# Attention with beacon tokens and a two-layer MLP on one core: products that nobody reads from the first microsecond, v loads that cast, x of one batch transposed by pairs

## The chip, the cores and the metric

The kernel runs on 1 core of one Trainium2 chip. The metric is the device time of one execution in microseconds (us), here from the first to the last thing that the core does for the program. Lower is better. TensorE (PE in the profile, PEld for its weight loads) multiplies, ScalarE (ACT) makes exponentials and copies, VectorE (DVE) and GpSimd (POOL) work elementwise, and DMA transfers are issued from the queues of SyncE (SP), ACT and POOL.

## What is computed

Inputs are float32. Attention runs over 8 batches (B) and 8 heads (H) with 576 queries (S) of width 64 (D). 16 beacon keys and values (Nb), which every query sees, stand ahead of the 576 causal ones. Its output goes through an MLP with a squared ReLU, 512 to 2048 to 512.

```python
k_all = np.concatenate([beacon_k, k], axis=2)
v_all = np.concatenate([beacon_v, v], axis=2)
scores = np.matmul(q, k_all.transpose(0, 1, 3, 2)) / np.sqrt(D)
scores = np.where(causal, -1000000000.0, scores)      # beacons are never masked
a = np.exp(scores - scores.max(-1, keepdims=True))
a /= a.sum(-1, keepdims=True) + 1e-09
x = np.matmul(a, v_all).transpose(0, 2, 1, 3).reshape(B * S, H * D)   # 4608 x 512
h = np.maximum(x @ w_in, 0.0)
out = (h * h) @ w_out
```

## The kernel before

**Tiling.** Heads go in pairs (`HP` = 4 pairs a batch, 32 in all), since two heads of 64 fill the 128 partitions of `qT` and `kT`. The 592 keys of a batch are five tiles (`NT`) of 128, the last of 80. For a pair, scores are made transposed (keys on the partitions) by L764 into PSUM, exponentials go by ACT into `pt` (L781), the diagonal is masked on DVE (L799, L803), and L819 multiplies with `vb`, which has a column of ones beside each head's v, so that the sum of a row comes with the product. DVE divides by it (`norm`, L834 and L835) into `xn`, tokens on the partitions. `xn` is transposed into `xT`, a ring of four batches with the 512 features on the partitions: batch 0 on TensorE with a copy behind (`add_xt_pe`, L883), all others by DMA transposes on SP (`add_xt`, L866), five a batch, each over one tile of tokens and all four pairs, after the norms of all four pairs.

**MLP.** Nine chunks of 512 tokens. First layer L947 (`s1`: 16 blocks of 128 hidden units, four products each), ReLU on ACT or DVE (L964, L966), square on DVE (L973); second layer L987 (`s2`, 16 products for each of four blocks of tokens), copy to `osb` by ACT, store on SP. Chunk 0 needs batch 0 alone, and its first layer is cut at token 240, so that the first two tiles of batch 0 can start it. Chunk 1 needs batch 1 as well.

**Loads.** k and q of batches 0 to 2 (`add_strided`) come by DMAs on POOL's queue that also cast to bf16 (L599), but for pair 0 of batch 0, which comes in float32 into space of `g` (L592). Each partition gets six neighbouring rows, so the data have to be turned: for batch 1, batch 2 and that first pair a copy (`spin`, on DVE; for the first pair on DVE or ACT) reorders a pair's k or q into `spare` or `qk_area`, then TensorE transposes (L635, L638) and DVE and ACT copy into `kT` and `qT` (`ek`, `eq`). Later batches use plain loads on SP, a cast on POOL and DMA transposes. v goes in float32 into one of eight staging tiles `stg` and is cast into `vb` (L439, on POOL but for two that may go to DVE); most of these loads go by SP, those in `SOFT_V` (batch 0's tiles 3 and 4, all five of batch 1) by POOL's queue (L483, L484). `w_in` (L908) and `w_out` (L917) come in four quarters each on POOL's queue, with a cast.

**The order.** The whole program is written out by a planner (`Order.run`, L155). Every piece of work is an `Op` with an engine or a choice of engines, a duration (by hand, in us), a priority, and what it needs. The planner walks through modelled time: an engine that is free takes the ready op of the least priority value for which PSUM banks (pool `ps`, eight) and other slots are free; DMA queues are modelled by packets (`Rings`). What it decides is each engine's instruction order and which engine takes an op with a choice; on the chip semaphores keep the needs, and each engine runs its list in order. `TURNS` (L306) fixes the order of POOL's loads. `gate` holds attention pairs of batch 1 and later back by the MLP's progress.

**Filler.** Where the planner finds nothing for PE between 10 and 22 us of its own time (`FILL`) and a bank is free, it adds two products of the identity `ident` into that bank, which nobody reads (`filler`, L526; in the trace L533 and L537). Their shape follows the mode of the op before: `rows` (64 rows, as the scores), `columns`, or full.

Of the kernel before, what the change touches and what calls it, by code (L numbers as in the profile page):

```python
# [129 lines left out]
class Order:  # L130
# [5 lines left out]
    FILL = (10.0, 22.0)  # L136
# [18 lines left out]
    def run(self):  # L155
# [27 lines left out]
        while events:  # L183
# [27 lines left out]
            while again:  # L211
                again = False
                for e in engines:
# [33 lines left out]
                    if best is None and e == "PE" and self.filler is not None and self.FILL[0] <= now < self.FILL[1]:  # L247
                        spot = self.pools["ps"].oldest()
                        if spot is not None:
                            best = self.filler(spot, mode or "full")  # L250
                            self.ops.append(best)
                            avail[e].append(best)
# [58 lines left out]
def kernel(  # L311
# [29 lines left out]
    def sb(name, shape, dt):  # L341
        return pool.tile(shape, dt, name=name)
# [21 lines left out]
    vb = [sb(f"vb{i}", [128, NT, H, D + 1], BF16) for i in range(2)]  # L364
# [19 lines left out]
    def act(n):  # L384
        return 0.066 + n / 1200.0
# [18 lines left out]

    nc.vector.memset(warm, 0.0)
# [46 lines left out]
    def t_start(t):  # L452
        return max(0, 128 * t - Nb)

    NPE = 3
    NXPE = 1
    SOFT_V = [(0, 3), (0, 4)] + [(1, c) for c in range(NT)]
# [10 lines left out]
    def add_load(b, x, c, prio, behind=[], sync=[]):  # L468
# [8 lines left out]
        queue = nc.gpsimd if soft else nc.sync  # L477

# [47 lines left out]
    def filler(spot, mode):  # L526


        def emit(e):
            for i in range(2):  # L530
                half = slice(64 * i, 64 * i + 64)
                if mode == "rows":
                    nc.tensor.matmul(ps[:, spot, 0:128], ident[0:64, :], ident[0:64, :], start=True, stop=True)  # L533
                elif mode == "columns":
                    nc.tensor.matmul(ps[half, spot, 0:128], ident[:, half], ident, start=True, stop=True)
                else:
                    nc.tensor.matmul(ps[:, spot, 0:128], ident, ident, start=True, stop=True)  # L537

        op = Op("fill", "PE", 0.11, emit, mode=mode)
        op.left, op.held = 0, None  # L540
        return op
# [38 lines left out]
    def add_strided(b, prio):  # L580
# [26 lines left out]
        for pr in range(HP):  # L607
# [34 lines left out]
            tp = add(f"tp{b}.{pr}", "PE", 0.55 if turned else 1.0, emit_tp, prio=100.0 * (HP * b + pr) - 190,  # L642
# [16 lines left out]
            eq = add(f"eq{b}.{pr}", ("DVE", "ACT"), {"DVE": 0.68, "ACT": 0.55}, emit_q, prio=-199.0, deps=[tp])  # L659
# [133 lines left out]
    def add_phase(b, pr, p, n, ph, take_pt, exps):  # L793
# [16 lines left out]
        def emit_av(e):  # L810
            P = pt[take_pt.held[0]]
            a = pair(av)
            for hj in range(2):
                h = 2 * pr + hj
                for t in tl:
                    for c in range(t + 1):
# [5 lines left out]
                            vb[b % 2][0:rr, c, h, :],  # L822
# [8 lines left out]
        def emit_norm(e):  # L831
# [4 lines left out]
                out=xn[b % 2].rearrange("p t (h d) -> p h t d", d=D)[:, 2 * pr:2 * pr + 2, tl[0]:tl[0] + nt],  # L836
# [8 lines left out]
        norm_ops[p, n] = add(f"norm{p}.{n}", "DVE", 0.21 + 0.137 * nt, emit_norm, prio=base - 150, deps=deps, give=av)  # L845
# [26 lines left out]

    def add_xt_pe(b):
        for k, ph in enumerate(phases(b)):
            for pr in range(HP):
# [14 lines left out]
                def emit_ev(e, pr=pr, box=box, lo=lo, hi=hi):  # L890
# [5 lines left out]
                        {"ACT": act(hi - lo), "DVE": 0.06 + (hi - lo) / 1600.0}, emit_ev, prio=-110.0,  # L896
# [164 lines left out]
    for b in range(B):  # L1061
# [32 lines left out]
        if b < NXPE:  # L1094
            add_xt_pe(b)
        else:
            add_xt(b)
# [12 lines left out]
    named["ld1v0"].behind.append(named["cast0v4"])  # L1110
# [32 lines left out]
```

## Time and profile before

| | |
|---|---|
| time, median of 3 runs | 338.75 us (338.75 to 340.36) |
| profiled execution | 338.65 us; span from first to last instruction 336.9 us |
| first matmul | 5.80 us after the span's start |
| first product of the MLP (L947) | 19.59 us |
| packets moved | 138211 DMA packets, 50.38 MB, mean 150 GB/s |
| q1 (SP's transfers) and q0 (POOL's) | 57.7% and 16.3% of 16 DMA engines' span |

The page gives for each engine its busy time; a busy PE is not PE at its peak, since matmuls overlap and their ends are modelled. A matmul's own length is therefore longer than the step from one to the next; how fast PE runs is read from the length of a run of equal matmuls. Times of rows count from the start of the span.

### The profile page before, as it was taken

Reading aid. Unit: us, or ns where it says so; the run is one execution under the profiler, and the core shown is the slowest. Engines: PE = TensorE matmul, PEld = TensorE weight load, DVE = VectorE, ACT = ScalarE, POOL = GpSimd, SP = SyncE. Lnnn points to the kernel's source line nnn. Section 1 sums busy time; section 2 is a strip of 40 time slices with the busy share of each in tenths; the row PEclk is TensorE's granted clock in tenths of the full one; section 3 lists DMA queues with packets and bytes.
Section 4 is the critical chain, followed back from the end, with each engine's and each line's share of the span. In section 5 each row is a group of like instructions: output and inputs, shape, how many; then the busy total and the mean of one; then the engine's idle time right before and its main releaser. Section 6 shows DMA issues by size and latency. Waiting matters only on the chain.

```text
span 336.9 us, 7692 instructions
## 1 busy us (share of the span) xinstructions
PE 327.1 (97%) x3172; PEld 184.2 (55%) x3172; DVE 160.5 (48%) x323; ACT 193.6 (57%) x300; POOL 86.8 (26%) x135
## 2 busy tenths in 40 slices
PE   3999999999999999999999999999999999999995
PEld 2778766545545555554468845545554544444444
DVE  6669977267604761475245632673246503301400
ACT  3887974597457647465656745755656226515611
POOL 7765911425122605140512351220000000000000
PEclk9999999999999999999999999999999999999999
DMA  9999999699959999799989996991310041011003
GB/s 167 196 207 210 206 203 207 147 247 179 221 104 223 241 199 176 185 208 228 206 121 257 242 210 138 209 196 32 104 62 2 14 120 63 0 62 64 0 17 110
DMA packets 138211, 50.38 MB, mean 150 GB/s; under 512 B 124176, under 2 KB 133264, under 8 KB 138176
## 3 DMA queue, kind: packets, MB, share of 16 engines
q1 hardware_dynamic: 128304, 40.42, 57.7%
q0 software_dynamic: 9520, 9.11, 16.3%
q8 instruction: 25, 0.41, 0.6%
q10 hardware_dynamic: 352, 0.36, 0.4%
q14 instruction: 10, 0.08, 0.1%
HBM read 37.22 MB, written 9.44 MB: 138 GB/s over the span
## 4 chain that ended last, share of the span: by engine, by line
PE 93%; DMA 2%; POOL 1%; DVE 1%; issue 1%; ACT 0%; POOLq 0%
PE ps L947 37%; PE ps L987 36%; PE ps L819 9%; PE ps L764 8%; DMA qk_area<-in_q_dram 2%; PE ps L635 1%; PE ps L1030 1%; POOL qk_area L599 1%; PE ps L883 1%; DVE g L966 0%; PE ps L537 0%; POOL vb L439 0%; PE ps L533 0%; POOL w_in L908 0%; DVE g L973 0%
## 5 line engine op out<-in xcount | busy, mean ns | idle before, releaser
L947 PE MATMUL ps<-xT,w_in 128*128 128x512 bf16 (+3 forms) x704 | 133.7, 340 | 0.2
L987 PE MATMUL ps<-w_out,g 128*128 128x512 bf16 x560 | 128.4, 379 | 0.0
L781 ACT ACTIVATE pt<-ps 128x1024 bf16<-128x1024 f32 (+3 forms) x128 | 102.9, 874 | 18.3 <-PE ps L764 18.1
L947 PEld LDWEIGHTS <-w_in 128*128 128x128 bf16 x704 | 65.9, 98 | 55.2 <-issue 3.9
L964 ACT ACTIVATE g<-ps 128x512 bf16<-128x512 f32 (+2 forms) x116 | 65.5, 568 | 39.1 <-PE ps L947 38.6
L987 PEld LDWEIGHTS <-g 128*128 128x128 bf16 x560 | 52.1, 98 | 61.1 <-issue 3.6
L973 DVE TENSOR_TENSOR g<-g 128x1024 bf16<-128x1024 bf16 (+2 forms) x80 | 52.1, 654 | 69.6 <-ACT g L964 69.4
L437 ACT COPY osb<-ps 128x512 f32<-128x512 f32 (+2 forms) x37 | 21.3, 576 | 68.8 <-PE ps L987 54.6
L439 POOL CAST qk_area<-stg 128x512 bf16<-128x512 f32 (+2 forms) x50 | 34.2, 688 | 67.5 <-DMA stg<-in_q_dram 41.0
L439 POOL CAST vb<-stg 128x512 bf16<-128x512 f32 (+1 forms) x39 | 26.1, 675 | 63.3 <-DMA stg<-in_v_dram 63.2
L799 DVE TENSOR_TENSOR pt<-pt,tri 128x1024 bf16<-128x1024 bf16 (+1 forms) x36 | 23.5, 654 | 34.2 <-ACT pt L781 34.2
L819 PEld LDWEIGHTS <-pt 128*128 128x128 bf16 (+1 forms) x960 | 34.2, 98 | 6.3 <-ACT pt L781 0.4
L966 DVE TENSOR_SCALAR g<-ps 128x512 bf16<-128x512 f32 (+2 forms) x44 | 26.8, 611 | 19.7 <-PE ps L947 19.4
L819 PE MATMUL ps<-vb,pt 128*128 128x65 bf16 (+1 forms) x960 | 35.6, 195 | 0.4 <-POOL vb L439 0.3
L764 PE MATMUL ps<-qT,kT 64*128 64x80 bf16 (+6 forms) x680 | 32.9, 235 | 0.0
L764 PEld LDWEIGHTS <-kT 64*128 64x128 bf16 x680 | 19.0, 96 | 16.8 <-issue 13.8
L835 DVE TENSOR_TENSOR xn<-ps,rcp 128x640 bf16<-128x640 f32 (+2 forms) x36 | 27.0, 750 | 1.8 <-DVE rcp L834 0.5
L834 DVE RECIPROCAL rcp<-ps 128x10 f32<-128x10 f32 (+2 forms) x36 | 7.5, 209 | 28.9 <-PE ps L819 28.9
L437 ACT COPY qT<-ps 128x576 bf16<-128x576 bf16 x12 | 7.6, 644 | 8.4 <-PE ps L635 7.4
L803 DVE TENSOR_TENSOR pt<-pt,tri 80x160 bf16<-80x160 bf16 x32 | 11.1, 347 | 0.0
L439 DVE COPY kT<-ps 128x576 bf16<-128x576 bf16 x12 | 8.9, 751 | 1.8 <-PE ps L638 1.2
L635 PE MATMUL ps<-ident,sparek 96*128 96x96 bf16 x18 | 1.5, 229 | 5.8 <-DVE sparek L439 5.8
(52 smaller groups left out, 80.4 us busy)
## 6 DMA issues: line engine op xcount, KB each, us to landing
out_dram<-osb SPq DMA_DIRECT2D x17, 512.0 KB, 3.6
stg<-in_v_dram SPq DMA_DIRECT2D x20, 256.0 KB, 5.1
stg<-in_q_dram SPq DMA_DIRECT2D x20, 256.0 KB, 5.5
stg<-in_k_dram SPq DMA_DIRECT2D x15, 256.0 KB, 4.3
w_in<-in_moe_w_in_dram POOLq DMA_DIRECT2D x4, 512.0 KB, 8.8
w_out<-in_moe_w_out_dram POOLq DMA_DIRECT2D x4, 512.0 KB, 11.6
stg<-in_v_dram SPq DMA_DIRECT2D x7, 224.0 KB, 4.5
qk_area<-in_k_dram POOLq DMA_DIRECT2D x4, 288.0 KB, 11.5
```

What stands on the lines that cost most here:

```text
L437: nc.scalar.copy(dst, src)
L439: eng[e].tensor_copy(dst, src)
L764: nc.tensor.matmul(st[:, hj, lo + col:lo + col + t1 - t0], kT[x.b % 2][hp, x.pr, 128 * c:128 * c + 128], qT[x.b % 2][hp, x.pr, t0:t1], sta ...
L781: nc.scalar.activation(pt[x.take_pt.held[0]][:, :, off:off + width], pair(box["qk"], k)[:, :, lo:lo + width], AF.Exp, bias=0.0, scale=scale)
L799: nc.vector.tensor_tensor(out=d, in0=d, in1=tri[:, m0:m0 + m, :][:, None].to_broadcast([128, 2, m, 128]), op=ALU.min)
L819: nc.tensor.matmul(a[:, hj, (t - tl[0]) * (D + 1):(t - tl[0] + 1) * (D + 1)], P[0:rr, hj, o:o + 128], vb[b % 2][0:rr, c, h, :], start=(c = ...
L835: nc.vector.tensor_tensor(out=xn[b % 2].rearrange("p t (h d) -> p h t d", d=D)[:, 2 * pr:2 * pr + 2, tl[0]:tl[0] + nt], in0=a[:, :, :, 0:D ...
L947: nc.tensor.matmul(h[:, lo - spans[0][0]:hi - spans[0][0]], w_in_sb[:, mc, ft * 128:(ft + 1) * 128], xT[:, mc, lo % RING:lo % RING + hi - lo],
L964: nc.scalar.activation(dst, h, AF.Relu, bias=0.0, scale=1.0)
L966: nc.vector.tensor_scalar(out=dst, in0=h, scalar1=0.0, scalar2=None, op0=ALU.max)
L973: nc.vector.tensor_tensor(out=d, in0=d, in1=d, op=ALU.mult)
L987: nc.tensor.matmul(o, G[:, fc, ts * 128:(ts + 1) * 128], w_out_sb[:, fc, :], start=(fc == 0), stop=(fc == NFT - 1))
```

## The change

1. `FILL` begins at 0.6 us of the planner's time. Before 2.6 us the filler is one product of 512 columns on `hot`, a part of `xT` set to zero by a memset that goes ahead of all others on DVE; it writes bank 7. After that it is the two products on `ident`, planned at 0.22 us before 6.0 us and at 0.11 us later. The form on 64 rows is gone: behind scores, it takes the full one.
2. Durations of the planner: ACT's copies and exponentials 0.105 + n / 1190 instead of 0.066 + n / 1200, the transposes of batch 0's pairs 0.55 instead of 1.0, `norm`, `eq` and `xte` by a few hundredths.
3. The loads in `SOFT_V` write bf16 straight into `vb`: no staging tile, no cast behind. A head's v and ones take 66 columns in `vb` instead of 65, of which L819 still reads 65. The rule that ties load 1v0 behind the cast of 0v4 goes with that cast.
4. Batch 1 (`XPAIR`): `xn` is laid out by pairs, and each pair's x is transposed after its own norm by three DMA transposes (tile 0, tiles 1 to 3, tile 4), twelve in all instead of five.
5. Batch 2's turning copies go to POOL instead of DVE, planned at 0.85 us instead of 0.45.

```diff
-    FILL = (10.0, 22.0)
+    FILL = (0.6, 22.0)
...
-    vb = [sb(f"vb{i}", [128, NT, H, D + 1], BF16) for i in range(2)]
+    vb = [sb(f"vb{i}", [128, NT, H, D + 2], BF16) for i in range(2)]
...
-        return 0.066 + n / 1200.0
+        return 0.105 + n / 1190.0
...
+    hot = xT[:, 0, 0:512]
+    nc.vector.memset(hot, 0.0)
     nc.vector.memset(warm, 0.0)
...
+        if soft:
+            def emit_soft(e):
+                to = vb[b % 2][:, c, :, 0:D]
+                insts = []
+                if lo:
+                    insts.append(queue.dma_start(out=to[0:Nb], in_=beacon[b].transpose([1, 0, 2])))
+                insts.append(queue.dma_start(out=to[lo:rows], in_=t[b, :, t0:t0 + rows - lo, :].transpose([1, 0, 2])))
+                return insts
+            ld = add(f"ld{b}{x}{c}", "POOL", 1.3 if lo else 0.65, emit_soft, prio=prio, dma=1.25 * rows / 128, packet=0.29,
+                     behind=load_chain[-1:] + behind, sync=sync)
+            load_chain.append(ld)
+            cast[b, x, c] = ld
+            return
...
-    def filler(spot, mode):
+    def filler(spot, mode, now):
+        mode = "columns" if mode == "columns" else "full"
+        if now < 2.6:
+            def emit(e):
+                nc.tensor.matmul(ps[:, 7, :], hot[:, 0:128], hot, start=True, stop=True)
+            op = Op("fill", "PE", 0.43, emit)
+            op.left, op.held = 0, None
+            return op
...
-                if mode == "rows":
-                    nc.tensor.matmul(ps[:, spot, 0:128], ident[0:64, :], ident[0:64, :], start=True, stop=True)
-                elif mode == "columns":
+                if mode == "columns":
...
-        op = Op("fill", "PE", 0.11, emit, mode=mode)
+        op = Op("fill", "PE", 0.22 if now < 6.0 else 0.11, emit, mode=mode)
...
-                    spin[x].append(add(f"spin{b}{x}{pr}", "DVE" if b else ("DVE", "ACT"), 0.45 if b else 0.85, emit_spin,
+                    spin[x].append(add(f"spin{b}{x}{pr}", ("POOL" if b == 2 else "DVE") if b else ("DVE", "ACT"), {"POOL": 0.85, "DVE": 0.45} if b else 0.85, emit_spin,
...
-            tp = add(f"tp{b}.{pr}", "PE", 0.55 if turned else 1.0, emit_tp, prio=100.0 * (HP * b + pr) - 190,
+            tp = add(f"tp{b}.{pr}", "PE", 0.55, emit_tp, prio=100.0 * (HP * b + pr) - 190,
...
-                out=xn[b % 2].rearrange("p t (h d) -> p h t d", d=D)[:, 2 * pr:2 * pr + 2, tl[0]:tl[0] + nt],
+                out=xn_of(b)[:, tl[0]:tl[0] + nt, pr, :].rearrange("p t (h d) -> p h t d", d=D),
...
+    def xn_of(b):
+        if b == XPAIR:
+            return xn[b % 2].rearrange("p t w -> p (t w)").rearrange("p (g t d) -> p t g d", g=HP, t=NT)
+        return xn[b % 2].rearrange("p t (g d) -> p t g d", g=HP)
+
+    def add_xt_pairs(b):
+        at = (b * S) % RING
+        for pr in range(HP):
+            for n, (lo, hi) in enumerate(((0, 1), (1, 4), (4, 5))):
+                t0, rows = t_start(lo), t_rows(lo)
+                cols = t_start(hi - 1) + t_rows(hi - 1) - t0
+                def emit(e, pr=pr, lo=lo, hi=hi, t0=t0, rows=rows, cols=cols):
+                    area = xn[b % 2].rearrange("p t w -> p (t w)")
+                    dst = xT[:, pr, at + t0:at + t0 + cols]
+                    if hi - lo > 1:
+                        dst = dst.rearrange("p (t r) -> p t r", r=rows)
+                    nc.sync.dma_start(out=dst, in_=area[0:rows, 128 * (NT * pr + lo):128 * (NT * pr + hi)], transpose=True)
+                o = add(f"xt{b}.{pr}.{n}", "SP", 0.55 + 0.19 * (hi - lo), emit, prio=-50.0 + b,
+                        deps=[norm_ops[HP * b + pr, 0]] + ring_deps(b * S + t0, b * S + t0 + cols), dma=0.16 * cols / 128,
+                        margin=1.0)
...
-            add_xt(b)
+            (add_xt_pairs if b == XPAIR else add_xt)(b)
...
-    named["ld1v0"].behind.append(named["cast0v4"])
```

More of the change, by code (lines that the diff above doesn't have):

```diff
@@ L249, in run @@
                         if spot is not None:
-                            best = self.filler(spot, mode or "full")
+                            best = self.filler(spot, mode or "full", now)
                             self.ops.append(best)
@@ L844, in add_phase @@
             deps += [o for (bb, _), o in xt_ops.items() if bb == b - 2]
[L845 removed]
+        norm_ops[p, n] = add(f"norm{p}.{n}", "DVE", 0.25 + 0.148 * nt, emit_norm, prio=base - 150, deps=deps, give=av)
     xt_ops = {}
@@ L895, in add_xt_pe @@
                 o = add(f"xte{b}.{k}.{pr}", ("ACT", "DVE"),
-                        {"ACT": act(hi - lo), "DVE": 0.06 + (hi - lo) / 1600.0}, emit_ev, prio=-110.0,
+                        {"ACT": act(hi - lo), "DVE": 0.1 + (hi - lo) / 1600.0}, emit_ev, prio=-110.0,
                         deps=[tp], give=tp)
```

7 lines of the change are left out of this document (5 added, 2 removed).

## The prediction

> **What bounds the kernel now.** I read the page's busy shares first, then the windows by stage, then the timelines of the first 30 us.
>
> ```profile
> PE 327.1 (97%) x3172; PEld 184.2 (55%) x3172; DVE 160.5 (48%) x323; ACT 193.6 (57%) x300; POOL 86.8 (26%) x135
> ```
>
> TensorE is the bound as an average. The windows (length, then busy time and instructions of PE, PEld, DVE, ACT, POOL, then PEclk, DMA share, GB/s) say where that does not hold:
>
> ```profile
> 5.80:17.80 12.00, 11.49 (x162) 8.79 (x164) 8.50 (x22) 8.84 (x14) 8.43 (x16) 1.00 1.08 195
> 8.00:28.00 20.00, 19.49 (x292) 14.63 (x289) 14.05 (x41) 16.21 (x25) 12.34 (x18) 1.00 1.15 201
> ...
> 36.00:40.00 4.00, 3.98 (x50) 3.14 (x47) 4.00 (x8) 4.00 (x10) 4.00 (x7) 1.00 1.18 198
> ...
> 48.00:88.00 40.00, 40.00 (x454) 22.09 (x453) 24.99 (x49) 25.90 (x40) 13.15 (x21) 1.00 1.05 200
> 88.00:333.50 245.50, 245.50 (x2127) 130.28 (x2123) 97.64 (x166) 130.83 (x199) 42.33 (x63) 1.00 0.63 133
> ```
>
> From 48 us PE never rests. So the end moves by the work that PE has behind it by about 48 us, its **lead**, plus what a new order costs or saves later. Before 48 us there are two stages: one to 28 us, and one around 36 to 40 us, where DVE and ACT are as full as PE.
>
> The first stage runs on a slow TensorE. The timeline of PE shows the same shapes early and late, and the chain of work (start, length) a stretch without pauses:
>
> ```profile
> 5.80 0.66 PE L635 MATMUL ps<-ident,sparek 96*128 96x96 bf16 x6 [5.80 <-DVE sparek L439]
> ...
> 14.92 0.85 PE L537 MATMUL ps<-ident 128*128 128x128 bf16 x6
> ...
> 17.98 0.72 PE L533 MATMUL ps<-ident 64*128 64x128 bf16 x10
> ...
> 32.06 0.42 PE L635 MATMUL ps<-ident,sparek 96*128 96x96 bf16 x6
> ```
>
> ```profile
> 305.84 13.84 PE ps L947 x64
> ```
>
> Six transposes take 0.66 us at 5.80 and 0.42 us at 32.06. Six 128-column products take 0.85 us at 14.92, ten of them 0.72 us at 17.98: 0.14 us each, then 0.07. In the dense stretch a 512-column product costs 13.84 / 64 = 0.216 us, so 128 columns at full rate cost about 0.054 us and at half rate 0.108. So TensorE runs at half rate until about 17.9 us, though the PEclk column reads 1.00. Half of the 11.49 us that PE was busy from 5.8 to 17.8 is 5.7 us: PE cannot gain more there.
>
> What an earlier full rate is worth is read from ScalarE, which makes every exponential of batch 0:
>
> ```profile
> 9.97 0.64 ACT L437 COPY qT<-ps 128x576 bf16<-128x576 bf16 x1 [0.30 <-PE ps L638]
> ...
> 16.76 0.36 ACT L437 COPY xT<-ps 128x240 bf16<-128x240 bf16 x1 [1.09 <-PE ps L883]
> 17.56 3.30 ACT L781 ACTIVATE pt<-ps 128x832 bf16<-128x832 f32 x4 [0.44 <-PE ps L764]
> ...
> 23.60 0.86 ACT L781 ACTIVATE pt<-ps 128x832 bf16<-128x832 f32 x1 [0.88 <-PE ps L764]
> ...
> 25.59 0.44 ACT L437 COPY xT<-ps 128x336 bf16<-128x336 bf16 x1 [0.53 <-PE ps L883]
> 25.93 1.94 ACT L781 ACTIVATE pt<-ps 128x928 bf16<-128x928 f32 x2
> ```
>
> Between 9.6 us and batch 0's last exponential, which ends at 27.87, ACT idles 0.30 + 1.09 + 0.44 + 0.88 + 0.53 = 3.24 us, each time until PE delivers. The window 8 to 28 gives 20.00 - 16.21 = 3.79 us idle in all. With an instant PE, ACT would still need the rest. So the lead at 28 us has a ceiling of 3.8 us, not 5.7.
>
> **Part 1: unread products from PE's first us.** Added on the path: one memset of `hot` (128x512 bf16) ahead of all on DVE. Rows for its price and for what it may delay:
>
> ```profile
> 1.57 0.27 DVE L410 MEMSET bks<- 128x256 uint32 x1
> ...
> 2.85 0.30 POOL masks.py:199 TENSOR_SCALAR_AFFINE_SELECT ident<-ident 128x128 bf16<-128x128 bf16 x1
> ...
> 5.19 0.56 DVE L439 CAST sparek<-g 96x768 bf16<-96x768 f32 x1 [1.05 <-DMA g<-in_k_dram]
> ```
>
> The memset has the bytes of the `bks` one: 0.27 us. DVE idles 1.05 us before 5.19, which covers it; without that cover it would be 0.27 us late. `ident` is made at 2.85 on POOL from a DVE memset that is done before 1.57 and would be done before 1.84, so it does not move. PE then has products from about 1.3 us: five of 512 columns at half rate (2 x 0.216 = 0.43 us each) to 3.4 us, then pairs on `ident` (ready 3.15) until the first transposes at 5.80, which wait for k's landing and do not move. A product that is still running when real work is ready costs one pair, 0.2 us, at most a few times; I charge it within what I leave of the 3.24 us.
>
> When does the rate rise? In the trace it rose only after a stretch with 128-row products in the gaps (14.9 to 17.9); transposes and scores with pauses, from 5.8, had not done it. The new stretch, 1.3 to 5.8 us, is 4.5 us without a pause, and the gaps behind it are filled too. I take 8 us or earlier.
>
> The Trainium skill ("TensorE: Matmul & The Clock Gate", Part 1, "What's actually happening") says that the clock is at half rate until one free-running window of about 3.4 us has been busy. By that alone the kernel before would have been at full rate by 5.8 + 6.8 = 12.6 us; its trace shows 0.14 us a product at 14.92, so it does not bear this out for work with pauses. For the new start the rule gives 4.7 to 8.1 us, and the same sum.
>
> ACT's three pauses before 17.9 (1.83 us) then go, and those at 23.60 and 25.59 shrink, since they come from PE's arrears. I take **2.8 us of the 3.24**; bounds 0 and 3.79. Next late is `w_in`, whose quarters gate the first layer:
>
> ```profile
> L908 POOL DMA_DIRECT2D w_in<-in_moe_w_in_dram x4: 768/771/777, 10.9 to 15.7; - x4
> ...
> DMA to landing us min/median/max: 7.2/8.8/11.5
> ```
>
> They land from 10.9 + 7.2 = 18.1 to 15.7 + 11.5 = 27.2 us. Nothing moves them, and so chunk 0's first layer ends behind 27.2 us whatever PE's rate; its last quarter and batch 1's scores are what PE has then.
>
> **Part 2: casting v loads.** Seven loads (0v3, 0v4, 1v0 to 1v4; 800 rows, as much as 6.25 full ones) write `vb` themselves; seven POOL casts go, and no cast stands between landing and use.
>
> ```profile
> L439 POOL CAST vb<-stg x5: 620/727/1068, 36.2 to 40.6; 128x512 bf16<-128x512 f32 x4, 80x512 bf16<-80x512 f32 x1
> ```
>
> ```profile
> 36.15 0.35 DVE L439 COPY qk_area<-qk_area 96x768 bf16<-96x768 bf16 x1
> ...
> 37.44 1.01 DVE L439 COPY qk_area<-qk_area 96x768 bf16<-96x768 bf16 x1
> ...
> 39.07 1.12 DVE L799 TENSOR_TENSOR pt<-pt,tri 128x1024 bf16<-128x1024 bf16 x1
> ```
>
> ```profile
> L799 DVE TENSOR_TENSOR pt<-pt,tri 128x1024 bf16<-128x1024 bf16 x28 | 20.0, 715 | 33.0 <-ACT pt L781 33.0
> ```
>
> The same DVE copy takes 0.35 us alone and 1.01 us beside these casts; the mask takes 1.12 us beside them against a mean of 0.72 us. That is 0.66 + 0.40 = 1.06 us of a DVE that is full from 36 to 40. I take **0.8 us**; bounds 0 and 1.06.
>
> The price is in the loads: each now writes 1024 pieces of 128 bytes. No row shows such a load. Queue shares and today's rate:
>
> ```profile
> q1 hardware_dynamic: 128304, 40.42, 57.7%
> q0 software_dynamic: 9520, 9.11, 16.3%
> ```
>
> ```profile
> L484 POOL DMA_DIRECT2D stg<-in_v_dram x5: 777/884/899, 24.9 to 30.8; - x5
> ...
> DMA to landing us min/median/max: 8.7/9.2/10.3
> ```
>
> Batch 1's v lands from 24.9 + 10.3 = 35.2 (its first load) to 30.8 + 8.7 = 39.5 us (its fifth): 464 rows in 4.3 us, 1.19 us per 128 rows. A packet of q1, 315 bytes on average, takes 0.577 x 336.9 x 16 / 128304 = 24 ns; of q0, 957 bytes, 92 ns. At 24 ns a load is 1024 x 24 / 16 = 1.55 us: 0.36 us more, 2.2 us over 6.25 loads. At 92 ns it is 5.9 us; if half the bytes meant half the time, 0.6 us less than now. I take 24 ns, since its packets are nearest in size. Everything behind on POOL's queue (`w_out`, batch 2's k and q) lands 2.2 us later.
>
> ```profile
> L987 PE MATMUL ps<-w_out,g x40: 376/379/390, 46.2 to 59.8; 128*128 128x512 bf16 x40
> L917 POOL DMA_DIRECT2D w_out<-in_moe_w_out_dram x4: 742/775/806, 32.0 to 35.5; - x4
> ...
> DMA to landing us min/median/max: 9.8/11.6/13.8
> ```
>
> The first quarter lands at 32.0 + 9.8 = 41.8 and is first used at 46.2. With a lead of 3.6 us the use would be at 42.6, the landing at 44.0: 1.4 us, over half of which PE fills with batch 1's other products. **Cost 0.6 us.**
>
> The skill ("DMA: Bandwidth & Descriptors", "Specifications") says that transfers under 512 B are read, modified and written. q1's loads, pieces of 256 bytes, show 24 ns under that rule already. If the narrower pieces doubled it to 48 ns, that is the second rival.
>
> **Part 3: batch 1's x by pairs, and the turning copies of batch 2 on POOL.**
>
> ```profile
> 58.99 6.50 SPq L866 DMA_TRANSPOSE xT<-xn  x5
> ...
> ```
>
> ```profile
> 57.00 1.24 POOL L439 CAST vb<-stg 128x512 bf16<-128x512 f32 x2 [13.83 <-DMA stg<-in_v_dram]
> ```
>
> ```profile
> 67.05 1.03 PE L947 MATMUL ps<-xT,w_in 128*128 128x512 bf16 x4
> 68.01 0.61 PE L764 MATMUL ps<-qT,kT 64*128 64x384 bf16 x8
> ...
> 73.73 1.09 PE L819 MATMUL ps<-vb,pt 128*128 128x65 bf16 x30
> ```
>
> SP issues five transposes in 6.50 us from 58.99, and the first reader starts at 67.05. Twelve smaller ones, three a pair, leave three after the last norm: at 1.30 us each as now 3.9 us, by their blocks (5 of 20) 1.6 us. So x is there 2.6 to 4.9 us earlier after its norm. PE did not wait for it, so this is worth 0; it keeps the lead from ending there, as it would from about 1.5 us on. The transposes share SP with batch 2's v loads; a transpose that waits for its norm holds these up, but v is first read at 73.73. The eight turning copies cost POOL, by its 0.73 us for a 512-wide cast, about 1 us each, 8 us in 51 to 62; it idles 13.83 us before 57.00. The casts of v2 behind them end near 64, still 9 us before 73.73. Without that cover it would be 2 to 4 us. Cost 0.
>
> **Part 4: measured durations in the planner** issue nothing; they move PE's order. Four products of 0.216 us at 67.05 last until 68.01, so one switch to scores costs about 0.1 us; ten switches more or fewer over eight batches are 1.0 us either way. I take 0.
>
> **Sum:** 2.8 + 0.8 - 0.6 = 3.0 us. The profiled execution took 338.65 us (span 336.9, 1.75 around it; the median of three runs is 338.75): 335.65, so **335.6 us**.
>
> **Rivals.** *The lead is given back before 48 us.* For it: DVE 4.00 and ACT 4.00 of 4.00 in 36 to 40, and batch 1's data do not land earlier, so a PE that is 3 us ahead only waits longer there. Against it: 1.06 us of DVE is freed, and PE has `w_out` from 44.0. Left: 0 to 1.5 us, 337.1 to 338.7; say 338.0. Chance 0.18.
>
> *Cast loads at 48 ns a piece.* A load takes 3.07 us, 1.88 us more; `v` of batch 1 and `w_out` come 11.8 us late.
>
> ```profile
> 41.71 1.08 PE L819 MATMUL ps<-vb,pt 128*128 128x65 bf16 x30
> ```
>
> PE's first product with that v stood at 41.71, with `w_out` at 46.2; from 42.8 on it had 3.4 us of work that needs neither. So v, landing at 39.5, could come 5.6 us late (45.1 = 41.7 + 3.4) before more than the lead is lost; beyond that the time itself goes: 338.65 + 11.8 - 5.6 = 344.9 us. It turns slower than before from (5.6 / 6.25 + 1.19) x 16 / 1024 = 33 ns a piece. For it: nothing in the page shows pieces this small; against: q1's 24 ns. Chance 0.08.
>
> *The first products do not raise the rate.* If it stays low until about 17.9 us, 0.8 - 0.6 remains: 338.4. Against it is the row pair around 17.9. Chance 0.06.
>
> *The new order switches more often or starves an engine late*, 1.5 us and more over the sum lost: 339 to 341, chance 0.04.
>
> **Chances.** Forecast 0.64 (332.7 to 337.0; lowest: 3.8 + 1.1 + 1.0 gained). Half a per cent, 1.7 us, is about what can be told from no change. Faster 0.64; within it 0.24 (first and third rival); slower 0.12. The range 332.7 to 339.2 leaves out the second rival, most of the fourth and a few per cent below.
>
> **What would show it.** Right: products at 1.3 us; 128 columns in 0.054 us by 8 us; ACT idle from 8 to 28 under 1.5 us; batch 0's last exponential ending near 25; no vb casts on POOL from 16 to 42; `w_out` first landing near 44; PE busy 4.00 of 4.00 from 40 on. Wrong: 0.108 us after 12 us; PE waiting at L819 or L987 near 43; `w_out` landing after 47.

## The result and the profile after

The changed kernel takes **340.08 us** (median of 20 runs, 338.14 to 342.33) against 338.96 us before (20 runs): ratio 1.0034, 95% interval 1.0018 to 1.0049. It is slower by 0.3%, where 335.6 us was forecast; the time lies above the range too. The profiled execution took 340.32 us (span 338.6) against 338.65 us (span 336.9): 1.7 us more.

The lines of the code move with the change: in the new kernel L790 makes the scores, L807 the exponentials, L845 the products with v, L661 and L664 the transposes of k and q, L935 those of batch 0's x, L892 and L917 the DMA transposes of x (by tiles, by pairs), L999 and L1039 the two layers, L551, L561 and L563 the unread products.

The page after: the busy shares have hardly moved, but the chain that ended last now holds SP's queue (SPq) and more DMA.

```profile
PE 327.7 (97%) x3168; PEld 185.4 (55%) x3209; DVE 156.1 (46%) x318; ACT 194.7 (57%) x298; POOL 88.3 (26%) x136
...
PE 84%; DMA 5%; SPq 3%; DVE 3%; issue 2%; ACT 1%; POOL 0%; POOLq 0%
```

The windows after, the same stretches as before (length, then busy time and instructions of PE, PEld, DVE, ACT, POOL, then PEclk, DMA share, GB/s):

```profile
5.80:17.80 12.00, 9.75 (x176) 6.96 (x173) 8.47 (x23) 9.45 (x14) 8.90 (x16) 0.79 1.32 192
8.00:28.00 20.00, 17.85 (x279) 13.00 (x276) 13.84 (x41) 16.20 (x25) 11.95 (x17) 0.83 1.31 199
```

ACT is busy for 16.20 us between 8 and 28 us, 16.21 before: nothing of its idle time was recovered. The clock column, 1.00 before (where it did not show the slow start), now falls below 1. Cut at the changes of the clock (a second answer of the same view):

```profile
9.00:12.60 3.60, 2.62 (x52) 1.72 (x51) 1.81 (x4) 3.60 (x7) 2.14 (x3) 1.00 1.17 226
12.70:19.40 6.70, 5.55 (x57) 3.68 (x57) 4.49 (x15) 4.47 (x7) 6.62 (x11) 0.50 1.42 180
19.60:28.00 8.40, 8.40 (x145) 6.71 (x143) 6.85 (x21) 6.83 (x12) 2.90 (x4) 1.00 1.28 204
```

TensorE was at full rate early, then ran dry (2.62 of 3.60 us busy), and **fell back to half rate from about 12.7 to 19.5 us**, later than it had been slow before (17.9). The rows agree with the column: four scores of 336 columns take 0.53 us at 16.10 and 0.35 us at 19.72. PE's timeline (start, length) shows the early rate and the pauses:

```profile
1.26 2.32 PE L551 MATMUL ps<-xT 128*128 128x512 bf16 x5 [1.26 <-DVE warm L407]
...
6.11 0.42 PE L661 MATMUL ps<-ident,sparek 96*128 96x96 bf16 x6
...
11.71 0.34 PE L790 MATMUL ps<-qT,kT 64*128 64x240 bf16 x4 [0.18 <-ACT qT L439]
12.40 0.27 PE L563 MATMUL ps<-ident 128*128 128x128 bf16 x2 [0.35 <-ACT pt L807]
```

The six transposes take 0.42 us at 6.11 instead of 0.66. But behind 9 us PE waits, mostly for ACT, and no unread product stands in the pauses: between 8 us and the L563 at 12.40 there is none. The planner puts one only where a bank is free. In its plan PE is repeatedly without ready work between 8.9 and 12.3 us, and no bank is free at any of these moments. Later ACT waits for PE again, by ACT's timeline:

```profile
16.20 0.36 ACT L439 COPY xT<-ps 128x240 bf16<-128x240 bf16 x1 [1.57 <-PE ps L935]
...
23.01 0.86 ACT L807 ACTIVATE pt<-ps 128x832 bf16<-128x832 f32 x1 [0.91 <-PE ps L790]
```

The second loss stands at 105 us, where PE stops for x of batch 2. Its timeline after:

```profile
104.41 0.84 PE L790 MATMUL ps<-qT,kT 64*128 64x256 bf16 x20
106.46 1.89 PE L999 MATMUL ps<-xT,w_in 128*128 128x512 bf16 x8 [1.21 <-DMA xT<-xn]
```

SP's timeline tells why, after:

```profile
94.39 2.42 SPq L503 DMA_DIRECT2D stg<-in_q_dram  x3
96.93 8.32 SPq L892 DMA_TRANSPOSE xT<-xn  x5
```

and SP's timeline before:

```profile
92.34 7.84 SPq L866 DMA_TRANSPOSE xT<-xn  x5
...
100.86 3.89 SPq L484 DMA_DIRECT2D stg<-in_q_dram  x4
```

In the new order three loads of batch 4's q stand ahead of batch 2's five transposes, which start 4.6 us later than before (96.93 against 92.34; about 3 us of it are these loads, since without them the transposes start at 93.97, in e2 below). The transposes also take 8.32 us. PE waits 1.21 us. At the last store the kernel is 1.6 us behind.

### The profile page after: what moved, and what is told of

It reads as the page before. It is cut to its first block, busy times and chain, and to the rows that moved or that the text cites. A ratio compares the mean times of both kernels' runs of the same rounds, so it can differ in the third digit from the quotient of the medians.

```text
span 338.6 us, 7727 instructions
## 1 busy us (share of the span) xinstructions
PE 327.7 (97%) x3168; PEld 185.4 (55%) x3209; DVE 156.1 (46%) x318; ACT 194.7 (57%) x298; POOL 88.3 (26%) x136
## 4 chain that ended last, share of the span: by engine, by line
PE 84%; DMA 5%; SPq 3%; DVE 3%; issue 2%; ACT 1%; POOL 0%; POOLq 0%
PE ps L999 35%; PE ps L1039 31%; PE ps L845 8%; PE ps L790 7%; DMA xT<-xn 2%; DMA stg<-in_v_dram 2%; DMA qk_area<-in_q_dram 1%; SPq L917 1%; PE ps L1082 1%; SPq L503 1%; DVE g L1018 1%; DVE pt L825 1%; SPq L892 1%; PE ps L563 1%; PE ps L661 1%
## 5 line engine op out<-in xcount | busy, mean ns | idle before, releaser
L999 PE MATMUL ps<-xT,w_in 128*128 128x512 bf16 (+3 forms) x685 | 133.2, 339 | 2.3 <-DMA xT<-xn 1.2
L1039 PE MATMUL ps<-w_out,g 128*128 128x512 bf16 x538 | 124.2, 379 | 1.4 <-issue 0.3
L807 ACT ACTIVATE pt<-ps 128x1024 bf16<-128x1024 f32 (+3 forms) x128 | 103.5, 873 | 37.2 <-PE ps L790 36.4
L999 PEld LDWEIGHTS <-w_in 128*128 128x128 bf16 x704 | 65.2, 98 | 55.3 <-issue 6.0
L1016 ACT ACTIVATE g<-ps 128x512 bf16<-128x512 f32 (+2 forms) x113 | 63.8, 565 | 46.0 <-PE ps L999 45.6
L1039 PEld LDWEIGHTS <-g 128*128 128x128 bf16 x560 | 52.7, 98 | 62.4 <-issue 3.2
L1025 DVE TENSOR_TENSOR g<-g 128x1024 bf16<-128x1024 bf16 (+2 forms) x80 | 51.0, 646 | 62.0 <-ACT g L1016 61.3
L825 DVE TENSOR_TENSOR pt<-pt,tri 128x1024 bf16<-128x1024 bf16 (+1 forms) x36 | 22.9, 636 | 41.5 <-ACT pt L807 41.5
L1018 DVE TENSOR_SCALAR g<-ps 128x512 bf16<-128x512 f32 (+2 forms) x47 | 28.5, 609 | 24.1 <-PE ps L999 22.4
L845 PEld LDWEIGHTS <-pt 128*128 128x128 bf16 (+1 forms) x960 | 34.1, 98 | 6.7 <-issue 1.2
L845 PE MATMUL ps<-vb,pt 128*128 128x65 bf16 (+1 forms) x960 | 35.4, 194 | 0.9 <-DVE vb L441 0.6
L441 POOL CAST vb<-stg 128x512 bf16<-128x512 f32 (+1 forms) x32 | 21.2, 672 | 48.3 <-DMA stg<-in_v_dram 44.3
L790 PE MATMUL ps<-qT,kT 64*128 64x80 bf16 (+5 forms) x680 | 32.3, 232 | 0.6 <-ACT pt L807 0.3
L790 PEld LDWEIGHTS <-kT 64*128 64x128 bf16 x680 | 18.5, 95 | 17.6 <-issue 15.0
L829 DVE TENSOR_TENSOR pt<-pt,tri 80x160 bf16<-80x160 bf16 x32 | 9.8, 308 | 0.0
L489 POOL DMA_DIRECT2D vb<-in_v_dram x7 | 5.9, 840 | 4.3 <-DMA w_in<-in_moe_w_in_dram 3.9
```

Of the source, the lines that this page charges most:

```text
L441: eng[e].tensor_copy(dst, src)
L790: nc.tensor.matmul(st[:, hj, lo + col:lo + col + t1 - t0], kT[x.b % 2][hp, x.pr, 128 * c:128 * c + 128], qT[x.b % 2][hp, x.pr, t0:t1], sta ...
L807: nc.scalar.activation(pt[x.take_pt.held[0]][:, :, off:off + width], pair(box["qk"], k)[:, :, lo:lo + width], AF.Exp, bias=0.0, scale=scale)
L825: nc.vector.tensor_tensor(out=d, in0=d, in1=tri[:, m0:m0 + m, :][:, None].to_broadcast([128, 2, m, 128]), op=ALU.min)
L845: nc.tensor.matmul(a[:, hj, (t - tl[0]) * (D + 1):(t - tl[0] + 1) * (D + 1)], P[0:rr, hj, o:o + 128], vb[b % 2][0:rr, c, h, 0:D + 1], star ...
L999: nc.tensor.matmul(h[:, lo - spans[0][0]:hi - spans[0][0]], w_in_sb[:, mc, ft * 128:(ft + 1) * 128], xT[:, mc, lo % RING:lo % RING + hi - lo],
```

## The experiments

All ratios are to the kernel before, run beside each group of experiments (medians 338.54 to 338.80 us), with 95% intervals. Each edit to the program makes the planner write the whole order anew, so that a difference holds the edit and the new order together; only what a trace shows as a wait is put down to one cause. Two theories were tested: the clock falls back since the planner has no bank for unread products while batch 0's scores hold all eight, and x of batch 2 comes late since the new order puts q loads ahead of it on SP. Rivals: Part 1 costs nothing and the other parts do, or the casting loads are dear.

**e1: Part 1 alone on the kernel before.**

```diff
-    FILL = (10.0, 22.0)
+    FILL = (0.6, 22.0)
...
+    hot = xT[:, 0, 0:512]
+    nc.vector.memset(hot, 0.0)
```

> The kernel before with part 1 alone (early unread products, the memset, no 64-row form). Theory A (TensorE at full rate waits for ScalarE with all eight PSUM banks taken, no unread product can be put there, and the clock falls back to half before 14 us): granted clock 0.5 again for 3.4 to 6.8 us somewhere between 9 and 20 us, mean clock 0.989 to 0.995, no lead at 67 us, 338.4 to 339.6 us, no wait over 0.5 us of L973 or its like for xT. Rival B (the clock holds and the lead is eaten by DVE and ACT around 36 to 44 us): mean clock 1.0, batch 0's last exponential before 26 us, 337.5 to 339. The forecast of 3 us from this part: 336.2 or less.

340.72 us, ratio 1.0064 (1.0038 to 1.0090). Its windows:

```profile
9.00:13.00 4.00, 2.33 (x56) 1.46 (x50) 1.08 (x3) 3.36 (x6) 2.52 (x4) 1.00 1.14 210
13.10:19.80 6.70, 5.39 (x56) 3.28 (x57) 5.60 (x18) 4.74 (x7) 6.03 (x10) 0.50 1.20 217
```

Without any of the other parts, too, a full rate is followed by a stretch in which PE is busy for only 2.33 of 4.00 us, and then by half rate. What ends the longest pause is another engine than in the changed kernel. PE's timeline:

```profile
11.42 0.35 PE L773 MATMUL ps<-qT,kT 64*128 64x336 bf16 x4 [0.27 <-ACT pt L790]
13.87 0.49 PE L773 MATMUL ps<-qT,kT 64*128 64x240 bf16 x4 [2.09 <-DVE kT L441]
```

PE pauses for 2.09 us until DVE has copied `kT`, 1.3 us of it ahead of the fall, and again no unread product stands there. The kernel with Part 1 alone is 2.0 us longer than before, above the range of Theory A. ACT is busy for 15.22 us between 8 and 28 us, so its idle time is 4.78 us, 1.0 us more than before; PE also waits for DVE later, 0.47 us at 39.44 and 0.44 us at 120.83. How much of the 2.0 us is the clock and how much the new order is not separated.

**e2: batch 4's q loads behind batch 2's x.**

```diff
+            elif b == 4 and n == 1:
+                behind = [xt_ops[2, t] for t in range(NT)]
```

> The changed kernel, with batch 4's first q load issued behind batch 2's five transposes of x. Theory A2 (the stop of 1.4 us at 105 us is these transposes standing behind three q loads on SP): the wait of L1001 for xT at 105 us goes, and the time with it, 1.2 to 1.6 us less than the changed kernel's 340.1: 338.5 to 338.9, ratio to before 0.999. Rival (the stop only moves, to the q loads' readers or the next chunk): 339.8 to 340.3, ratio 1.003.

338.84 us, ratio 1.0005 (0.9985 to 1.0025), 0.3% below the changed kernel's 1.0034. SP's timeline shows the edit, and PE's wait for x is gone:

```profile
93.97 6.43 SPq L892 DMA_TRANSPOSE xT<-xn  x5
```

The clock still falls back as in the changed kernel (0.50 from 12.4 to 19.1 us). The late x is one cause and not the whole.

What the fall itself costs can be read without a new order, since executions of one program differ in it. In the changed kernel, e1 and e2 some executions have a mean clock of 0.993 to 0.995, the others, which lost more of it, 0.980 to 0.990. The medians are 339.89 us (8 executions) against 340.24 (12) in the changed kernel, 340.40 (3) against 341.37 (9) in e1, and 338.25 (7) against 339.66 (5) in e2: 0.3, 1.0 and 1.4 us less where less of the clock was lost. The groups overlap, so the size is rough, and it is not shown that data which land later do not make both.

**e3: a PSUM bank kept for unread products until 22 us of the plan.**

```diff
-        self.free = set(range(8))
+        self.free = set(range(7))
...
+            if self.KEPT is not None and now >= self.FILL[1]:
+                self.pools["ps"].give(1, self.KEPT)
+                self.KEPT = None
...
-                        spot = self.pools["ps"].oldest()
+                        spot = self.KEPT
```

> The changed kernel, with PSUM bank 7 kept out of the pool for the first 22 us of the plan, so that an unread product can be put wherever PE has nothing. Theory A: clock 1.0 from its first rise to the end, ACT idle from 8 to 28 us 2.5 us or less (3.8 in both kernels), batch 0's last exponential ends by 26.5; a lead of 1 to 2.5 us at 67 us (first L999-like product of chunk 1 at 64.5 to 66); with the stop at 105 left in, 338 to 339.5 us. Rival B (what ends batch 0 is landing and ACT, whatever the clock): clock 1.0 but no lead, 340 us. Rival C (one bank less starves ACT): ACT idle from 8 to 28 over 4.5 us, 341 us.

338.07 us, ratio 0.9993 (0.9975 to 1.0012). The window of the first stage:

```profile
8.00:28.00 20.00, 20.00 (x371) 15.87 (x366) 14.62 (x44) 17.50 (x29) 12.08 (x17) 1.00 1.31 200
```

PE's timeline of the same kernel in the stretch that had run dry:

```profile
11.17 0.62 PE L567 MATMUL ps<-ident 128*128 128x128 bf16 x8
11.72 0.37 PE L794 MATMUL ps<-qT,kT 64*128 64x208 bf16 x4
12.03 0.40 PE L567 MATMUL ps<-ident 128*128 128x128 bf16 x4
```

(L567 and L794 are this kernel's unread products and scores.) Every gap between scores is filled, PE is busy for all 20.00 us, the clock stays at 1.00, and ACT is busy 17.50 us, so its idle time is 2.50 instead of 3.80. That confirms the first theory. PE does not wait for x of batch 2 here either, although SP has q loads ahead of it. SP's timeline:

```profile
90.67 5.42 SPq L507 DMA_DIRECT2D stg<-in_q_dram  x4
96.19 7.35 SPq L896 DMA_TRANSPOSE xT<-xn  x5
```

So the q loads alone do not make the wait; they take the margin. Before, SP had issued the last of these transposes 4.9 us ahead of the first product of the chunk that reads them (100.18 against 105.04); here it is 0.1 us (103.54 against 103.64). In the changed kernel the same five transposes took 8.32 us instead of 7.35, and that showed as a wait. Why they took 1 us longer there is not shown.

**e4: both edits**, those of e2 and e3.

> Both edits: bank 7 kept for unread products until 22 us of the plan, and batch 4's q loads behind batch 2's transposes of x. Theories A and A2 together: 336.5 to 338 us, ratio 0.993 to 0.997, no PE wait over 0.5 us behind 25 us. If the clock is worth nothing: as the second run, 338.5 to 338.9. If both fall: 340.

337.89 us, ratio 0.9976 (0.9952 to 1.0000): the lowest time of the study, 0.85 us under the 338.74 of before beside it, but not to be told from e3's. The time lies in the range that was expected, the ratio just outside it. ACT's idle time from 8 to 28 us is 20.00 - 16.86 = 3.14 us. Against e2, which has the same order on SP and a clock that falls, it is 0.95 us shorter. Against the changed kernel's 1.0034 the two repairs bring 0.6%; against before the change then gains about a quarter of a per cent, at the edge of what can be told, of 0.9 forecast.

**e5: the change without Part 1.**

```diff
-    FILL = (0.6, 22.0)
+    FILL = (10.0, 22.0)
...
-    hot = xT[:, 0, 0:512]
-    nc.vector.memset(hot, 0.0)
```

> The changed kernel without part 1 (fill from 10 us on, old filler, no memset): parts 2 to 5 alone. If part 1 is what costs (its run alone stood 2 us over the kernel before, at a clock that fell back), parts 2 to 5 gain: rate low until 17 to 18 us as before, then no fall; 337.3 to 338.5 us without a stop at batch 2's x, 338.5 to 339.3 with one. Rival: parts 2 to 5 cost too, 340 us or more. Landing by the casting loads as in the changed kernel: first quarter of w_out at 40 to 41 us.

338.60 us, ratio 1.0012 (0.9988 to 1.0036). PE does not wait for x, although three q loads stand ahead of batch 2's transposes here too (94.77; the transposes from 97.25 us, in 7.29 us). The clock column reads 0.91 from 8 to 28 us, about 3.6 us at half rate, where no fall was expected. So Parts 2 to 5, with a TensorE that is not at full rate through the first stage, are worth nothing that can be measured.

**e6: e4's kernel with float32 v loads and POOL casts** (Part 2 undone).

```diff
-        if soft:
+        if soft and False:
```

> The kernel of the fourth run (bank kept, q loads behind x; 337.9 us) with part 2 undone: float32 v loads into staging and casts on POOL. Theory: the casting loads are cheaper, not dearer (0.7 us per 128 rows against 1.2 in the kernel before, by the landings of the changed kernel); undone, w_out's first quarter lands 1 to 2 us later (41.5 to 42.5) and the casts slow DVE again: 338.3 to 339.3 us. Rival (the landing is covered by other work of PE): 337.6 to 338.1.

339.77 us, ratio 1.0038 (1.0021 to 1.0055), against e4's 0.9976: with the casting loads (and the order that goes with them) the kernel is 0.6% faster. PE's timeline shows where most of it is lost:

```profile
37.50 0.62 PE L1003 MATMUL ps<-xT,w_in 128*128 128x272 bf16 x4 [0.79 <-DVE g L1022]
...
40.46 0.43 PE L665 MATMUL ps<-ident,qk_area 96*128 96x96 bf16 x6 [0.50 <-DVE qk_area L445]
```

PE waits 0.79 + 0.50 = 1.29 us for DVE, where e4 has no such wait. DVE's turning copy takes 1.21 us at 35.89, beside POOL's casts of v; in the changed kernel one takes 0.34 us at 39.02, and the mask 0.68 us at 39.64. `w_out` is not the reason: its first quarter lands at 31.1 + 9.1 = 40.2 us, not at 41.5 to 42.5 as expected. The prices of the loads can be compared too (us from issue to landing). The view of the tile `vb` in the changed kernel:

```profile
L489 POOL DMA_DIRECT2D vb<-in_v_dram x5: 737/888/896, 24.1 to 29.5; - x5
...
DMA to landing us min/median/max: 7.5/8.4/10.3
```

The view of `stg` in e6:

```profile
L507 POOL DMA_DIRECT2D stg<-in_v_dram x5: 739/882/897, 24.0 to 29.9; - x5
...
DMA to landing us min/median/max: 8.0/8.8/9.9
```

The changed kernel's loads land from 24.1 + 10.3 = 34.4 to 29.5 + 7.5 = 37.0 us, 464 rows in 2.6 us, 0.72 us per 128 rows; e6's from 33.9 to 37.9, 1.10 us. A load that writes half the bytes takes two thirds of the time here, and three fifths of the 1.19 us of the kernel before.

**e7: e4's kernel with batch 1's x transposed as before.**

```diff
-    XPAIR = 1
+    XPAIR = -1
```

> The same kernel with part 4's transposes undone: batch 1's x by five transposes after the last norm. Theory (a lead of 1 to 1.5 us ends at this x, read first at 66 us): the first product of chunk 1 waits or stands 1 us or more later, 338.7 to 339.7 us. Rival (the plan orders other work ahead, nothing lost): 337.6 to 338.2; or twelve transposes cost more than five: 337.3.

339.12 us, ratio 1.0023 (1.0003 to 1.0042). PE's timeline where chunk 1 begins:

```profile
68.66 0.39 PE L794 MATMUL ps<-qT,kT 64*128 64x384 bf16 x4 [0.83 <-ACT pt L811]
69.57 0.40 PE L794 MATMUL ps<-qT,kT 64*128 64x256 bf16 x4 [0.52 <-ACT pt L811]
69.90 2.41 PE L1003 MATMUL ps<-xT,w_in 128*128 128x512 bf16 x9
```

The plan has x later here and puts scores ahead of chunk 1, and these wait 0.83 + 0.52 us for exponentials. With the pairs (e4) chunk 1 begins at 65.96. So the pairs keep a lead from being lost here. How much of the 1.2 us between e7 and e4 this is stays open: the profiled execution (340.99 us) is the slowest of the twelve, and PE waits in it for other things too, 0.88 us at 28.09 for beacon keys and 0.43 us at 59.16 for `kT`.

**e8: e4's kernel with batch 2's turning copies on DVE.**

```diff
-("POOL" if b == 2 else "DVE") if b else
+"DVE" if b else
```

> The same kernel with batch 2's turning copies back on DVE. Theory (no engine is short at 50 to 62 us): 337.6 to 338.2 us. Rival (the copies on POOL delay v2's casts, which free the staging tiles for SP's loads; on DVE these loads come 2 us earlier): 337 to 337.5. Rival (DVE is short): 338.5 or more.

339.26 us, ratio 1.0014 (0.9992 to 1.0036); the interval overlaps with e4's. PE waits again, this time for x of batch 1. PE's timeline, then SP's:

```profile
68.03 1.25 PE L1003 MATMUL ps<-xT,w_in 128*128 128x512 bf16 x4 [0.88 <-DMA xT<-xn]
```

```profile
62.03 0.73 SPq L507 DMA_DIRECT2D stg<-in_q_dram  x1
62.86 4.70 SPq L921 DMA_TRANSPOSE xT<-xn  x3
```

The three transposes of the last pair start at 62.86 and take 4.70 us; in e4 they start at 61.89 and take 3.72 us. A q load stands ahead of them that e4 has behind them. DVE is not short, as one rival had it: it is busy for 7.35 of 12 us from 48 to 60. So what this run shows is again a wait by the order on SP; a price of the copies themselves does not show in it.

**e9: Part 1 with its bank on the kernel before**, q loads behind x as in e2.

> The kernel before with Part 1 alone, PSUM bank 7 kept for the unread products until 22 us of the planner's time, and batch 4's first q load behind batch 2's five x transposes. If the clock falling back is what Part 1 alone lost by (340.72 us), the clock column shows 1.00 from about 6 us on, ScalarE idles about 2.5 us instead of 4.8 between 8 and 28 us, and the time is 337.3 to 338.4 us, ratio 0.996 to 0.999. Rival: the held clock is worth nothing without the casting loads, since GpSimd's casts and w_out end last around 40 us anyway: 338.5 to 339.2 us, ratio 0.999 to 1.001, with a lead at 28 us that is gone by 48 us.

344.18 us, ratio 1.0141 (1.0096 to 1.0186). The numbers of both theories missed by far. PE's timeline:

```profile
11.07 0.84 PE L550 MATMUL ps<-ident 128*128 128x128 bf16 x12
14.07 0.33 PE L777 MATMUL ps<-qT,kT 64*128 64x240 bf16 x4 [2.15 <-DVE kT L445]
```

The windows of the same kernel (L550 are its unread products, L777 its scores):

```profile
36.00:39.00 3.00, 1.08 (x27) 0.74 (x19) 2.96 (x6) 2.47 (x3) 3.00 (x6) 1.00 1.21 196
39.10:42.40 3.30, 3.18 (x28) 2.38 (x29) 1.49 (x3) 2.16 (x4) 2.73 (x5) 0.50 1.24 205
```

The number of unread products in a gap is fixed by the plan. Twelve stood in this one; PE ran them in 0.84 us, and `kT` came 2.15 us later than that. The clock fell to half from 15.1 to 18.5 us. It fell a second time at 39 us, where PE had 1.08 us of work in 3 us beside a DVE and a POOL that were full (2.96 and 3.00). Of six executions the one with a mean clock of 0.999 took 340.84 us, that with 0.994 341.60, and the four with 0.989 or 0.990 344.08 to 345.63. A kept bank alone is thus not enough. Even the execution that kept the clock is 2.3 us above the 338.54 of before, so this order costs by itself; why was not followed.

**e10: e4's kernel with the planner's former durations** (Part 4 undone).

```diff
-        return 0.105 + n / 1190.0
+        return 0.066 + n / 1200.0
```

> The kernel with the bank kept and the q loads behind x (337.89 us), with the planner's former durations (Part 4 undone). If the durations are worth 0 within 1.0 us, as the prediction has it: 337.0 to 338.7 us, and no single wait of TensorE over 0.5 us behind 88 us. Rival: the new durations give an order that the chip follows better, so the old ones cost over 1 us: 339 us and above, with TensorE waiting for ScalarE or a bank between 28 and 88 us.

338.43 us, ratio 0.9996 (0.9973 to 1.0019), which overlaps with e4's. Here the durations are worth what was assumed: 0 within 1 us.

**e11: e4's kernel with bank 7 given back at 16 us of the plan.**

```diff
-            if self.KEPT is not None and now >= self.FILL[1]:
+            if self.KEPT is not None and now >= 16.0:
```

> The kernel with the bank kept and the q loads behind x (337.89 us), but bank 7 given back at 16 us of the planner's time instead of 22. If the clock needs the bank only while the scores of batch 0 hold the other seven: clock 1.00 throughout, and 337.4 to 338.1 us. Rival: the clock falls back behind about 18 us of the trace, since there the banks are taken again: 0.5 for 3 to 7 us in the record and 338.4 to 339.5 us.

338.73 us, ratio 1.0010 (0.9993 to 1.0027). The clock stays at 1.00, as the theory has it, but the time is the rival's. The order differs from 16 us of the plan on, and the difference from e4 was not traced to one wait.

**e12: Part 4 alone on the kernel before.**

```diff
-        return 0.066 + n / 1200.0
+        return 0.105 + n / 1190.0
```

> The kernel before with Part 4 alone (the planner's durations). If Part 4 moves only the order and costs by the place where it puts transfers: here the planner has batch 2's x transposes ahead of batch 4's q loads, so TensorE does not wait for x at 105 us and the time is 338.2 to 339.3 us, ratio 0.998 to 1.002. Rival: the durations by themselves give a worse order: 340 us and above, ratio over 1.003, with a stop of over 0.5 us behind 60 us.

340.21 us, ratio 1.0046 (1.0029 to 1.0064). The theory's range missed, and the rival's holds. The clock is not the cause: its column stays at 1.00. A stop as at batch 2's x in the changed kernel stands at batch 1's, 35 us earlier, and again q loads stand ahead of x. SP's timeline:

```profile
58.99 3.05 SPq L484 DMA_DIRECT2D stg<-in_q_dram  x3
62.13 7.64 SPq L866 DMA_TRANSPOSE xT<-xn  x5
```

PE's timeline of the same kernel:

```profile
70.00 0.39 PE L764 MATMUL ps<-qT,kT 64*128 64x256 bf16 x4 [0.55 <-ACT pt L781]
70.92 1.02 PE L947 MATMUL ps<-xT,w_in 128*128 128x512 bf16 x4 [0.52 <-ACT pt L781]
```

Three q loads are issued at 58.99, where the kernel before has its x transposes; these come 3.1 us later (SP has issued the last at 69.77 instead of 65.49), PE has only scores that wait 0.55 + 0.52 us, and chunk 1 begins at 70.92 instead of 67.05. The new durations and the order that goes with them cost 1.7 us on this kernel, and 1.1 us of waits stand at this place. PE also waits 0.35 us at 27.52 for beacon keys and 0.37 us at 39.97 for DVE. The profiled execution (339.48 us) is the fastest of the six.

## Why the prediction was wrong

**Part 1 is the step that failed.** The first half of its argument held: the products start at 1.26 us, and TensorE is at full rate by 6.11, ahead of the 8 us assumed. The sentence "the gaps behind it are filled too" did not hold. The row of a free bank, which decides whether an unread product can stand in a gap, was never looked up; nor was it asked what a TensorE at twice the rate does when its work comes from ACT: it runs out sooner. It ran dry from 9 to 12.6 us and lost the clock for about 6.8 us. Instead of 2.8 us of ACT's idle time none came back (3.80 against 3.79). That is shown by e1 (the fall without the other parts, around a gap without a product), by e3 and e4 (no fall with a bank kept), and by e9 (a fall with the bank, where the gap outlasted its products).

The size was wrong as well. With the clock held ACT's idle time fell by 1.3 us (e3; in e4 by 0.65), not by 2.8. The pause of 0.88 us at 23.60, put down to PE's arrears, is still there at full rate. ACT's timeline in e3:

```profile
22.23 0.86 ACT L811 ACTIVATE pt<-ps 128x832 bf16<-128x832 f32 x1 [0.80 <-PE ps L794]
```

PE was busy all through this stretch: it did other work first, by the order that the planner wrote.

**Part 2 had the wrong sign at its price.** 24 ns a piece, 1.55 us a load, was taken; 0.72 us was measured, or 0.72 x 16 / 1024 = 11 ns a piece. The bound "half the bytes, half the time" was the near one; the packets of SP's queue were no guide. The Trainium skill ("DMA: Bandwidth & Descriptors", "Specifications") has transfers under 512 B read, modified and written, which was the second rival; no price of that kind shows in these loads. `w_out` did not come 2.2 us later, by the view of that tile after:

```profile
L969 POOL DMA_DIRECT2D w_out<-in_moe_w_out_dram x4: 742/754/762, 32.3 to 34.9; - x4
...
DMA to landing us min/median/max: 7.7/10.2/13.4
```

Its first quarter lands at 32.3 + 7.7 = 40.0 us, 1.8 us earlier than before; e6 has it at 40.2 with float32 loads, so this cannot be put down to the casting loads. The 0.6 us of cost were not there. The freed DVE (0.8 us) was rightly counted as a gain: a copy and the mask are as short in the changed kernel (0.34 and 0.68 us) as the prediction has them without casts beside, and without Part 2 PE waits 1.29 us for DVE (e6). But in the changed kernel there was no lead to keep.

**Part 3 held** as far as the runs show: no wait is put down to the pairs or to POOL's copies, and without the pairs chunk 1 starts later (e7).

**The new order, costed under Part 4 at 0 within 1 us by TensorE's switches alone, cost 1.2 us by SP's queue** (at 105 us; e2). "They issue nothing" is true of the durations, but the transfers on SP move with the order, and the effect on a queue was not asked for. The durations on the kernel before cost 1.7 us, with a stop of the same kind (e12); with the q loads tied behind x they are worth 0 (e10). That the durations made the order at 105 us is not shown: the planner puts three q loads ahead of x in the changed kernel without Part 4, too, and e5, without Part 1, has them. Nor does the order make a wait each time: e3 and e5 have it without one, with next to no margin. The fourth rival, a new order that starves an engine late, names this mechanism, and 0.04 was too small a chance for it. That the time also falls into its 339 to 341 us is partly luck, since the wait is 1.2 of the 4.7 us between forecast and measurement.

**The sum.** Forecast -3.0 us, measured +1.7 in the profiled execution. The twenty scores that PE makes ahead of the chunk with batch 2's x cut each profiled execution in two:

| | before | changed | e2 | e3 | e4 | e5 |
|---|---|---|---|---|---|---|
| start of these scores, us | 104.27 | 104.41 | 104.06 | 102.87 | 103.28 | 103.57 |
| span, us | 336.9 | 338.6 | 337.0 | 335.8 | 336.2 | 336.5 |
| from that start to the end, us | 232.6 | 234.2 | 232.9 | 232.9 | 232.9 | 232.9 |

Up to there the changed kernel has no lead but is 0.1 us behind, where 3.0 us ahead were forecast, 2.8 of them by Part 1. Behind it stand the 1.2 us of the wait and 0.3 us that e2 to e5 lose as well, whose cause was not followed. With the bank kept the lead is 1.4 us (e3) and 1.0 us (e4), against 0.2 us in e2 with the clock falling. These are single executions, but the medians of e4 and e2 agree (0.95 us). The rest of the forecast did not come in any of these orders.

## What to carry to other kernels

Work that only keeps TensorE's clock up has to reach into every gap until the real work is dense, with a PSUM bank of its own and enough of it for the longest gap on the chip, not in the plan; a clock that rises early and falls back can leave nothing of the gain (ACT's idle time was 3.80 us against 3.79 with the late rise, and 4.78 in e1). When the durations of a planner change, compare the order on every queue, SP's first: a load ahead of a transpose of something that is needed soon takes its margin, which was 4.9 us before and 0.1 us in e3, and one slow transfer then becomes a wait. An engine's pause that ends with another engine's work isn't worth that engine's speed: look whether it was busy with something else.

## What the runs showed of the hardware

The clock can fall back without a long pause. In the changed kernel no pause of PE between its first product and the fall at 12.66 us is longer than 0.35 us, and PE counts as busy for 2.62 of 3.60 us. In e1 it was 2.33 of 4.00 us, with a pause of 2.09 us that began 1.3 us ahead of the fall. In e9 a pause of 2.15 us stood ahead of it. The Trainium skill ("TensorE: Matmul & The Clock Gate", "HAM oscillation — how this bites in real kernels") gives as rule that no gap should exceed about 3.4 us; these falls came with shorter ones. The Trainium skill ("TensorE: Matmul & The Clock Gate", "A second HAM failure mode: psum-queue depth-cycling") also tells of a clock that oscillates from many small pauses, which the changed kernel's rows agree with.

A DMA transpose keeps SP busy for nearly the same time over one tile as over three. The view of `xT` after, with batch 1's twelve (ns: min, median, max):

```profile
L917 SPq DMA_TRANSPOSE xT<-xn x12: 1093/1252/2552, 43.4 to 66.5; - x12
```

Eight of the twelve are over one tile and four over three; the median is 1.25 us, as for the five larger ones of before (6.50 us for five). Of the prediction's two bounds for them, 1.30 us and a share by blocks, the first was right.
